# Attention products of a linear-attention and MLP layer: pairs of token tiles in six PSUM banks

## The chip, the core and the metric

The kernel runs on one core of one Trainium2 chip. The metric is device time in microseconds (us). A core has five engines, each with a queue of its own that it works off in order: TensorE (PE in the profile) multiplies matrices into PSUM, ScalarE (ACT) and VectorE (DVE) do elementwise work and are the ones that read PSUM here, GpSimd (POOL) does elementwise work in SBUF, and SyncE (SP) issues the DMAs. PSUM is used as eight banks of 512 fp32 values per partition. The TensorE clock that the profile shows as granted is 1.000 of full speed over the span.

## What is computed

For a sequence of 2048 tokens of 640 features in bf16 the layer adds three things: the input, a linear attention with 32 heads of 20 features, and a gated MLP with 1536 hidden features. Both branches work on the normalized input.

```python
xn = layernorm(x)
q, k, v = heads(xn @ wqkv)                      # 32 heads of 20
phi(u) = [softmax(u @ w_phi), softmax(-u @ w_phi)]   # 40 features per head
kv  = sum over s of phi(k)[s] x v[s]            # 40 x 20 per head
z   = sum over s of phi(k)[s]
o   = (phi(q) @ kv) / (phi(q) . z + 1e-6)
out = x + o @ wo + (silu(xn @ w1) * (xn @ w3)) @ w2
```

## The kernel before

The tokens lie in 16 tiles of 128 (`T`) and four batches of 512 (`NB`). The work on TensorE is cut into units. A unit is a group of matmuls that fills one, two or four neighbouring PSUM banks, followed by the ACT and DVE operations that empty them:

- `v_tile` and `k_tile` (two banks each) make v and exp(plus and minus k) of a token tile, `k_norm` divides the latter by their sums on DVE and POOL, and `kv_sum` and `kv_back` make the matrix of all heads, `KVc`. `KVc` holds 22 columns per head for each sign (`sg`): 20 for the numerator and two for the denominator.
- `q_proj` (one bank, five 512-wide matmuls) makes `EqT`, exp(plus and minus q) of 128 features of a batch, transposed, with two ACT operations.
- `q_tok(t)`, the attention product of token tile t, fills four banks. It runs on half of the array's rows at a time: 20 matmuls of 64 rows and 88 columns. Two with different row halves (`r`) go side by side into different banks. The loops run over sign, over five chunks `c` of the features, and over `r`; bank number 2 x sg + r. ACT then copies the two denominator columns of each head to `e_s` in two operations. DVE makes the products of the parts (`pr_s`), their sum (`den_s`), its reciprocal and the factors `g_s`; one multiply of 1280 elements weights all four banks into `prod`, and that is the last reader of the banks. A further sum gives `o_tok`, which a DMA transposes into `oT` (`turn`). Buffers `e_s`, `pr_s`, `den_s`, `g_s` and `prod` are there twice, by t % 2. A unit may not start before the last multiply of the one before (`u.behind`).
- `mlp(b, fc)` (two banks, 20 matmuls 512 wide) makes 128 hidden features of a batch: ACT makes tanh (`th`), and DVE makes `t1` and `hT` with one operation each.
- `out_tile(t)` (two banks) sums 12 chunks of `hT` by w2 and five of `oT` by wo into the two halves of an output row, 34 matmuls 320 wide. One DVE operation over both banks adds them to `xres`, which holds x, and a DMA stores it. The last tile is cut into 384 and 256 columns instead.

The order of the work is not written out by hand. `schedule` plans it before the program is built: it keeps a clock for each engine, gives every operation a duration (`w_act`, `w_tt` and the like), and takes next the unit or operation that can start earliest. Within a slack the higher level wins; `when(us)` turns a wished time into a level. A unit whose array form differs from that of the one before (`mode`: full rows, rows in halves, columns in halves) is charged `MODE`, 0.085 us. With a seed, and up to 175 us of the plan, the slack is drawn at random, so another seed gives another order. `bank_time` and `group_time` say when banks have been emptied, and `fit` chooses between free ones. A unit of four banks that could start soon keeps others from taking its banks (`blocked`). `emit` then turns the planned order into one list per engine, with waits on semaphores.

Two parts of one unit can be planned apart: `v_split` opens a second unit whose `anchor` is the first one, so that it goes on in the same banks. `emit` numbers the semaphores and lets an output store wait for the fourth store before it.

In the run before, the products of all 16 tiles lie between 117.9 and 202 us of the span. Up to about 165 us `mlp` and `q_proj` units lie between them, from there on one output unit after each product. The last batch's `mlp` units fill 225 to 251 us, and four output units end the span. The load of w2 is issued at 107 us, after the last reader of the memory it takes, and that of wo at 57 us.

Memory that the change touches: `e_s` lies in `RV` behind `oT`, `prod` and `o_tok` in `RW` behind `KVc`.

Of the kernel before, what the change touches and what calls it, by code (L numbers as in the profile page):

```python
# [10 lines left out]
D = 640  # L11
H = 32
# [8 lines left out]

ENGINES = ("PE", "ACT", "DVE", "POOL", "SP")
SEM = {"PE": 0.06, "ACT": 0.04, "DVE": 0.04, "POOL": 0.08, "SP": 0.05}
MODE = 0.085
GRAN = 8
BACKLOG = 5.0

# [28 lines left out]
class _Unit:  # L56


    def __init__(self, banks, level, mode):
        self.banks, self.level, self.mode, self.k = banks, level, mode, None  # L60
        self.mms = []
        self.first = {}
        self.readers = [[] for _ in range(banks)]
        self.behind = []
        self.anchor = None
        self.name = ""


class _Program:
# [100 lines left out]


    def schedule(self, start, filler=None, filler_until=0.0, seed=None, shaken=0.0):
        rng = random.Random(seed)

        for n, o in enumerate(self.all):
            o.idx = n
# [32 lines left out]
        bus = 0.0  # L209
        issue = {"ACT": start["ACT"]}  # L210
        queues = {"SP": [], "ACT": []}
        mode = "full"
        owner = [None] * 8
        ready = {e: [] for e in ENGINES}
        ready_u = [u for u in self.units if not u.missing]
# [113 lines left out]
        def group_time(u, k, guess=False):  # L329
            return max(bank_time(k + j, u.first[j].off if j in u.first else 0.0, guess) for j in range(u.banks))  # L330

        def fit(k, n, t):

            if n == 4:
                return 0
            size = 2 * n
            base = k // size * size
            return sum(1 for i in range(base, base + size) if not k <= i < k + n and bank_time(i, 0.0, True) <= t)
# [3 lines left out]
        while left:  # L342
            best = None
            pick = None
            if ready_u:
                t0 = free["PE"]
                slack = 0.12 if seed is None or t0 > shaken else rng.choice((0.03, 0.12, 0.12, 0.3, 0.6))
                blocked = set()
                cands = []
                for u in ready_u:  # L350
                    extra = MODE if u.mode != mode else 0.0
                    u.at = max(unit_time(u), t0 + extra)
                for u in sorted(ready_u, key=lambda u: (-u.level, u.mms[0].idx)):
                    opts = [(u.at, 0, u.anchor.k)] if u.anchor is not None else []
                    for k in range(0, 8, u.banks) if u.anchor is None else ():
                        if blocked & set(range(k, k + u.banks)):
                            continue
                        g = group_time(u, k)
                        if g < 1e8:
                            opts.append((max(g, u.at), fit(k, u.banks, u.at), k))  # L360
                    if opts:
                        x = min(opts)
                        if pick is None or x[0] < pick[0] - slack:
                            pick = (x[0], u, x[2])
                    if u.banks == 4 and u.at <= t0 + 1.0 and not blocked and (not opts or x[0] > u.at + 0.03):
                        k = min((group_time(u, k, True), k) for k in (0, 4))[1]
                        blocked |= set(range(k, k + 4))
                if pick is not None:
                    best = (pick[0], "PE", pick[1], pick[2])
            moved = False  # L370
            for e in ("ACT", "DVE", "POOL", "SP"):
# [1 line left out]
                    continue  # L373
                ts = [(max(issue[e] if o.nbytes and e == "ACT" else free[e], op_time(o, e)), o) for o in ready[e]]
                t = min(x[0] for x in ts)
                w = 0.09 if seed is None or t > shaken else rng.choice((0.03, 0.09, 0.09, 0.2, 0.4))
                t, o = min((x for x in ts if x[0] <= t + w), key=lambda x: (-x[1].level, x[1].idx))
                if len(o.ways) > 1 and o.level > 1.5e6:
                    other = min(max(free[f], op_time(o, f)) + o.ways[f][2] for f in o.ways if f != e)
# [11 lines left out]
            if e == "PE":  # L391
# [22 lines left out]
                if t > t0 + 0.03 + (MODE if x.mode != mode else 0.0):  # L414
                    self.gaps.append((t0, t - t0, x.name))
                x.k = k
                mode = x.mode
                ready_u.remove(x)
                for j in range(x.banks):
                    p = owner[k + j]  # L420
# [73 lines left out]
CENTRED = {0: "ACT", 1: "ACT", 2: "DVE"}  # L494
POOLED = ()
TURNED = ()
SEED = 1138
TRIPLES = ((0, 3, 0, 60), (3, 3, 60, 60), (6, 3, 120, 60), (9, 3, 180, 60), (12, 3, 240, 60), (13, 3, 300, 20))


def bass_parallel_sum__linear_kernel_hedgehog__glu_gated_swiglu__prompt_kernel(
# [26 lines left out]
    def new(name, shape, dtype, offset=None):  # L528
        size = mybir.dt.size(dtype)
        for n in shape[1:]:  # L530
            size *= n
        return P.sbuf(name, shape, dtype, region(size) if offset is None else offset)
# [9 lines left out]
    mv = new("mv", [128, T, 8], f32)  # L542
    mhalf = new("mhalf", [128, 4], f32)
    warm = new("warm", [128, 8], f32)
    pr_s = new("pr_s", [128, 2, 2, H], f32)
    den_s = new("den_s", [128, 2, H], f32)
    g_s = new("g_s", [128, 2, 2, H], f32)
    S64 = new("S64", [128, 3, 64], f32)
    rS64 = new("rS64", [128, 3, 64], f32)
    xnT = new("xnT", [128, DC, S], bf)  # L550
# [31 lines left out]
    RV = region(21568)  # L582
    v2 = new("v2", [128, T, H * 21 + 2], bf, RV)
    oT = new("oT", [128, DC, S], bf, RV)
    e_s = new("e_s", [128, 2, 4, H], f32, RV + 20480)

    RW = region(12800)
    wqkT = new("wqkT", [128, 2 * DC, D], bf, RW)
    KVc = new("KVc", [128, 2, DC, 4 * 22], bf, RW)
    prod = new("prod", [128, 2, 2, D], bf, RW + 1760)  # L590
    o_tok = new("o_tok", [128, 4, D], bf, RW + 6880)
    kvT = new("kvT", [128, 2, 320], bf, RW + 6880 + 3840)
    EqT = [EqT0, EqT1]
# [4 lines left out]
    def bank(k, cols=512, off=0, p0=0, p1=128):  # L598
        return PS[p0:p1, k * 512 + off:k * 512 + off + cols]
# [62 lines left out]
    def w_op(eng, name, args, busy, lat, **kw):  # L662
        return way(eng, name, args, kw, busy, lat)
# [336 lines left out]
    turned = []  # L1000

    def q_tok(t, level):
        b, jj = divmod(t, 4)
        u = P.begin(4, level, "row", "qt")
        u.name = f"qt{t}"
        u.behind.extend(turned[-1:])
        for sg in range(2):
            for c in range(DC):
                for r in range(2):
                    j = 2 * sg + r  # L1010
                    mm(j, lambda k, j=j, c=c: bank(k + j, 88, 66 * c),
                       EqT[b % 2][64 * r:64 * r + 64, sg, c, 128 * jj:128 * jj + 128],
                       KVc[64 * r:64 * r + 64, sg, c, :], c == 0, c == DC - 1, True,
                       0.003 if r == 0 else 0.045)

        def ps(k):
            a = PS[:, k * 512:(k + 4) * 512].rearrange("p (n c) -> p n c", c=512)[:, :, 0:352]
            return a.rearrange("p n (h c) -> p n h c", c=22)
        e = e_s[:, t % 2, :, :]
        up = 2e6  # L1020
        for sg in range(2):
            o = e[:, sg:4 - sg:3 - 2 * sg, :]
            add([w_act(o.rearrange("p c (q h) -> p q h c", h=16),
                       lambda k, sg=sg: ps(k)[:, 2 * sg:2 * sg + 2, :, 20:22], ACT.Copy, 64)],
                [e], [], [2 * sg, 2 * sg + 1], up)
        pr, den, g = pr_s[:, t % 2, :, :], den_s[:, t % 2, :], g_s[:, t % 2, :, :]
        add([w_tt("DVE", pr, e[:, 0:2, :], e[:, 2:4, :], ALU.mult, 64)], [pr], [e], None, up)
        add([w_tt("DVE", den, pr[:, 0, :], pr[:, 1, :], ALU.add, 32)], [den], [pr], None, up)
        add([w_op("DVE", "reciprocal", (den, den), 0.27, 0.36)], [den], [den], None, up)
        add([w_tt("DVE", g, e[:, 2:4, :], den.unsqueeze(1).to_broadcast([128, 2, 32]), ALU.mult, 64)],  # L1030
            [g], [e, den], None, up)
        gq = g.rearrange("p s (q h) -> p (s q) h", h=16)
        p2 = prod[:, t % 2, :, :]
        add([w_tt("DVE", p2.rearrange("p s (q h c) -> p (s q) h c", q=2, c=DH), lambda k: ps(k)[:, :, :, 0:DH],
                  gq.unsqueeze(3).to_broadcast([128, 4, 16, DH]), ALU.mult, 1280)],
            [p2], [g], [0, 1, 2, 3], up)
        turned.append(P.all[-1])
        o = o_tok[:, t % 4, :]
        add([w_tt("DVE", o, p2[:, 0, :], p2[:, 1, :], ALU.add, D, 2)], [o], [p2], None, 5e5)
        turn(oT[:, :, t * 128:(t + 1) * 128], o, 1e5 - t)  # L1040

    nmlp = [0]

# [18 lines left out]
    def out_tile(t, level):  # L1062
        b, ti = divmod(t, 4)
        u = P.begin(2, level, stream="O")
        u.name = f"O{t}"
        chunks = [(hT[b][:, i, ti * 128:(ti + 1) * 128], w2_s, i) for i in range(FC)]
        chunks += [(oT[:, i, t * 128:(t + 1) * 128], wo_s, i) for i in range(DC)]
        r = xres[:, t % 4, :].rearrange("p (b c) -> p b c", c=320)
# [2 lines left out]
            P.all[-1].early = 60.0  # L1071
        if t < T - 1:
            for n, (l, w, i) in enumerate(chunks):
                for q in range(2):
                    mm(q, lambda k, q=q: bank(k + q, 320), l, w[:, i, 320 * q:320 * q + 320], n == 0,
                       n == len(chunks) - 1)
            add([w_tt("DVE", r, lambda k: bank2(k, 320), r, ALU.add, D)], [xres[:, t % 4, :]],
                [xres[:, t % 4, :]], [0, 1], 1e6)
            finish.append(load(out_t[:, t, :], xres[:, t % 4, :], 3e5 - 2 * t))
            return  # L1080
        for q, c0, c1 in ((0, 0, 384), (1, 384, D)):
# [92 lines left out]
    def when(us):  # L1174
        return 1000.0 - us
# [30 lines left out]
    for b in range(NB):  # L1206
        for j in range(4):
            t = 4 * b + j
            q_tok(t, when(110 + t))
            if b + 1 < NB:  # L1210
                for fc in range((5 * j + 3) // 4, (5 * j + 8) // 4):
                    q_proj(b + 1, fc, when(110 + t + 0.1 * fc))
    for t in range(T):
        out_tile(t, when(200 + 5 * t))

# [62 lines left out]
```

The softmax here doesn't subtract the row's maximum and nothing guards it: scores larger than these inputs give would overflow.

## Time and profile before

| | us |
|---|---|
| median of five runs | 273.76 (273.36 to 273.97) |
| the profiled execution | 273.76 |
| its span, first to last instruction | 272.0 |
| DVE busy, 117 to 128 us | 9.30 of 11 |
| DVE busy, 152 to 164 us | 10.92 of 12 |
| ACT busy, 117 to 128 us | 7.17 of 11 |
| DVE `prod`, 1280 elements, x16 | 1.491 each |
| DVE sum of an output tile, 640 elements, x15 | 0.825 each |
| DVE reciprocal of 64 elements (`rS`), of 32 (`den_s`) | 0.535, 0.353 |
| ACT `e_s`, 64 elements, x32 | 0.283 each |
| transpose of one `o_tok`, from issue to landing | 2.6 |

A profile row for a matmul shows its whole passage through the array, and neighbours overlap: a 512-wide matmul lasts 379 ns, while the next starts 215 to 216 ns after it. What a stretch of matmuls costs is therefore read from the starts. `PEld` rows are the weight loads that run beside them. In a row of the timeline, several instructions of a kind are merged: its first column is the first start, its second the time from there to the last end. An engine's idle time before a row and what ended it stand in brackets.

### The profile page before, as it was taken

To read this page: it belongs to the slowest core of one execution; us is meant where nothing else is said; L and a number is where in the kernel's file an instruction comes from. 1 tells how busy PE (TensorE), PEld (TensorE's weight loads), DVE (VectorE), ACT (ScalarE), POOL (GpSimd) and SP (SyncE) were. 2 spreads that over 40 slices of the span, in tenths; PEclk is the share of its full clock that TensorE was granted. 3 is DMA by queue.
4 is the path that set the end of the run, shared out by engine and by line. 5 is a ranking of instruction groups with operands and counts; after the bars stand their busy time and mean duration, and the time that the engine had idled before them with its cause. 6 is when DMAs were issued, how large, how long until landed. Compare 5 with 4: busy or idle time off the path is not lost.

```text
span 272.0 us, 5056 instructions
## 1 busy us (share of the span) xinstructions
PE 267.4 (98%) x2080; PEld 159.8 (59%) x2098; DVE 182.6 (67%) x325; ACT 101.8 (37%) x190; POOL 60.9 (22%) x101
## 2 busy tenths in 40 slices
PE   8999999999999999999999999999999999999996
PEld 5746546777754448444444446777677774444774
DVE  4848989999998453688869994777673215666112
ACT  5535826777754541355583354100110002222000
POOL 4320642789999900000000000000000000000000
PEclk9999999999999999999999999999999999999999
DMA  7668996863000000804031111333353122000001
GB/s 222 216 98 281 355 164 122 101 164 126 0 0 2 0 0 10 285 0 50 1 51 24 24 27 29 95 99 98 95 100 86 62 77 70 0 0 0 27 24 48
DMA packets 39975, 21.98 MB, mean 81 GB/s; under 512 B 27024, under 2 KB 39952, under 8 KB 39952
## 3 DMA queue, kind: packets, MB, share of 16 engines
q1 hardware_dynamic: 39376, 21.01, 32.4%
q10 hardware_dynamic: 576, 0.66, 0.7%
q8 instruction: 16, 0.26, 0.4%
q14 instruction: 7, 0.06, 0.1%
HBM read 12.81 MB, written 2.62 MB: 57 GB/s over the span
## 4 chain that ended last, share of the span: by engine, by line
PE 94%; DVE 2%; ACT 2%; issue 1%
PE PS L619 92%; PE PS L1098 2%; ACT EqT L627 2%; DVE t L627 1%; PE PS L814 0%; DVE hT L627 0%; PE PS L867 0%; DVE den_s L627 0%; DVE prod L627 0%; ACT e_s L627 0%; DVE g_s L627 0%; DVE xres L627 0%; DVE o_tok L627 0%; DVE pr_s L627 0%
## 5 line engine op out<-in xcount | busy, mean ns | idle before, releaser
L619 PE MATMUL PS<-xnT,w_s 128*128 128x512 bf16 x465 | 104.6, 379 | 1.0 <-issue 0.3
L619 PEld LDWEIGHTS PS<-xnT,w_s 128*128 128x128 bf16 x480 | 46.5, 98 | 54.7
L627 ACT ACTIVATE th<-PS 128x512 f32<-128x512 f32 x48 | 28.7, 597 | 72.0 <-PE PS L619 71.9
L619 PE MATMUL PS<-w_s,hT 128*128 128x320 bf16 (+2 forms) x384 | 55.0, 299 | 0.0
L627 DVE SCALAR_TENSOR_TENSOR t<-th,PS 128x512 bf16<-128x512 f32 x48 | 32.7, 683 | 27.5 <-ACT th L627 27.5
L619 PEld LDWEIGHTS PS<-w_s,hT 128*128 128x128 bf16 x384 | 37.0, 98 | 14.9
L627 POOL TENSOR_TENSOR ekt<-ekt,rS 128x640 bf16<-128x640 bf16 x32 | 39.4, 1264 | 1.1 <-DVE rS L627 1.1
L627 DVE TENSOR_TENSOR xres<-PS,xres 128x640 bf16<-128x640 f32 (+2 forms) x17 | 13.3, 785 | 37.8 <-PE PS L619 37.8
L627 DVE SCALAR_TENSOR_TENSOR hT<-t,PS 128x512 bf16<-128x512 bf16 x48 | 32.7, 684 | 1.3
L627 ACT ACTIVATE EqT<-PS 128x512 bf16<-128x512 f32 x40 | 21.9, 594 | 11.8 <-PE PS L619 11.7
L619 PE MATMUL PS<-wo_s,oT 128*128 128x320 bf16 (+2 forms) x160 | 24.5, 299 | 0.0
L627 DVE TENSOR_TENSOR prod<-PS,g_s 128x1280 bf16<-128x1280 f32 x16 | 23.9, 1491 | 0.6
L627 ACT ACTIVATE ekt<-PS 128x640 bf16<-128x640 f32 x32 | 20.8, 701 | 9.0 <-PE PS L619 8.8
L619 PE MATMUL PS<-Wkp,xnT 128*128 128x320 bf16 x160 | 23.9, 299 | 0.0
L627 ACT ACTIVATE e_s<-PS 128x64 f32<-128x64 f32 x32 | 9.1, 283 | 38.2 <-PE PS L619 37.7
L619 PE MATMUL PS<-xnT,Wqp 128*128 128x512 bf16 x97 | 22.9, 379 | 0.3 <-ACT EqT L627 0.2
L627 DVE TENSOR_REDUCE S<-ekt 128x64 f32<-128x1280 bf16 x16 | 22.9, 1447 | 0.0
L619 PE MATMUL PS<-wv,xnT 128*128 128x320 bf16 x130 | 19.8, 299 | 0.0
L619 PEld LDWEIGHTS PS<-wo_s,oT 128*128 128x128 bf16 x160 | 15.7, 98 | 6.1
L619 PEld LDWEIGHTS PS<-Wkp,xnT 128*128 128x128 bf16 x160 | 15.5, 98 | 5.9
L619 PEld LDWEIGHTS PS<-xnT,Wqp 128*128 128x128 bf16 x100 | 9.4, 98 | 11.0
L627 DVE BATCH_NORM_STATS2 bst<-x_tok 128x6 f32<-128x320 bf16 x32 | 14.1, 469 | 2.6 <-DMA x_tok<-in_A_x_dram 2.6
(66 smaller groups left out, 164.4 us busy)
## 6 DMA issues: line engine op xcount, KB each, us to landing
w_s<-in_B_w_dram SPq DMA_DIRECT2D x6, 640.0 KB, 6.8
xres<-in_A_x_dram SPq DMA_DIRECT2D x16, 160.0 KB, 2.3
out_dram<-xres SPq DMA_DIRECT2D x15, 160.0 KB, 1.8
x_tok<-in_A_x_dram SPq DMA_DIRECT2D x3, 640.0 KB, 8.2
w_s<-in_B_w_dram SPq DMA_DIRECT2D x1, 1920.0 KB, 9.0
wo_s<-in_A_wo_dram SPq DMA_DIRECT2D x1, 800.0 KB, 5.2
x_tok<-in_A_x_dram SPq DMA_DIRECT2D x2, 160.0 KB, 3.6
x_tok<-in_A_x_dram ACTq DMA_DIRECT2D x2, 160.0 KB, 4.0
```

The costliest lines, as they stand in the source:

```text
L619: return nc.tensor.matmul(o(u.k), l, r, start=start, stop=stop, skip_group_check=shared)
L627: return getattr(e, name)(*[at(a, u) for a in args], **{k: at(v, u) for k, v in kw.items()})
L1098: return nc.tensor.matmul(bank(u.k, n), ones[:, 0:128], ones[:, 0:n], start=True, stop=True)
```

## The change

The change has five parts.

1. `q_tok` handles two neighbouring token tiles and is called for every second one. It fills six banks: for tile m of the pair, the bank 2 x r + m holds 23 heads of row half r (16 of one sign and 7 of the other), and the remaining 9 heads of both tiles lie in bank 4 + r. So a chunk of features in which the heads change banks is cut into 22 and 66 columns, and a pair of tiles takes 44 matmuls instead of 40. ACT copies the denominator columns in three operations (128, 56 and 72 elements), DVE makes each small step once for both tiles (`g_s` in two), and three multiplies of 920, 920 and 720 elements each empty two banks. The buffers for these steps are there once. The sums and the transposes stay one per tile.
2. The planner places six banks at 0 to 5 or 2 to 7. Right after a unit of six banks (`wide`) it prefers units that are marked `long`, which are the output units.
3. The output unit of tile 0 (`PARTED`) is planned in two parts: 24 matmuls by w2, and then, in the same banks, ten by wo.
4. The sum of an output tile is two DVE operations of 320 elements, one for each bank, instead of one of 640.
5. `MODE` is 0.096. The levels of `q_tok`, and of the `q_proj` units that are planned with it, go from `when(110 + t)` to `when(118 + 2.5 * t)`. The random draws follow seed 1138 up to 45 us, as before, and seed 597 from there.

```diff
-MODE = 0.085
+MODE = 0.096
...
+        def places(n):
+            return range(0, 9 - n, n if n < 4 else 8 - n)
+
         def fit(k, n, t):
 
-            if n == 4:
+            if n >= 4:
                 return 0
...
-                for u in sorted(ready_u, key=lambda u: (-u.level, u.mms[0].idx)):
+                for u in sorted(ready_u, key=lambda u: (-u.level - (1e7 if wide and u.long else 0), u.mms[0].idx)):
...
-                mode = x.mode
+                mode, wide = x.mode, x.banks == 6
...
-SEED = 1138
+SEED = ((0.0, 1138), (45.0, 597))
+PARTED = (0,)
...
     def q_tok(t, level):
+
         b, jj = divmod(t, 4)
-        u = P.begin(4, level, "row", "qt")
+        u = P.begin(6, level, "row", "qt")
         u.name = f"qt{t}"
         u.behind.extend(turned[-1:])
+        seen = set()
         for sg in range(2):
-            for c in range(DC):
-                for r in range(2):
-                    j = 2 * sg + r
-                    mm(j, lambda k, j=j, c=c: bank(k + j, 88, 66 * c),
-                       EqT[b % 2][64 * r:64 * r + 64, sg, c, 128 * jj:128 * jj + 128],
-                       KVc[64 * r:64 * r + 64, sg, c, :], c == 0, c == DC - 1, True,
-                       0.003 if r == 0 else 0.045)
...
+            for m in range(2):
+                for c in range(DC):
+                    parts = ((0, 4),) if not sg or c != 2 else ((0, 1), (1, 4))
+                    for lo, hi in parts:
+                        for r in range(2):
+                            h = 3 * c + lo
+                            j, off = (4 + r, 256 * m + 22 * (h - 7)) if sg and h >= 7 else (2 * r + m, 22 * (16 * sg + h))
+                            first = j not in seen
+                            seen.add(j)
+                            n = 22 * (hi - lo)
+                            mm(j, lambda k, j=j, n=n, off=off: bank(k + j, n, off),
+                               EqT[b % 2][64 * r:64 * r + 64, sg, c, 128 * (jj + m):128 * (jj + m) + 128],
+                               KVc[64 * r:64 * r + 64, sg, c, 22 * lo:22 * hi], first,
+                               sg == 1 and (c == 2 and hi == 1 if j < 4 else m == 1 and c == DC - 1), True,
+                               0.003 if r == 0 else max(0.024, n / 2400))
...
+        for r in range(2):
+            o, i = prod[:, 2 * r:2 * r + 2, 0:23, :], g_s[:, 2 * r:2 * r + 2, 0:23]
+            add([w_tt("DVE", o, lambda k, r=r: big(k)[:, 2 * r:2 * r + 2, :, 0:DH],
+                      i.unsqueeze(3).to_broadcast([128, 2, 23, DH]), ALU.mult, 920)], [o], [i], [2 * r, 2 * r + 1], up)
+        o, i = prod[:, :, 23:32, :], g_s[:, :, 23:32]
+        add([w_tt("DVE", o, lambda k: rest(k)[:, :, :, 0:DH], i.unsqueeze(3).to_broadcast([128, 4, 9, DH]), ALU.mult,
+                  720)], [o], [i], [4, 5], up)
         turned.append(P.all[-1])
...
+        u.long = True
...
+                if n == FC and t in PARTED:
+                    P.begin(0, u.level).name = f"O{t}b"
+                    P.unit.anchor = u
...
-            add([w_tt("DVE", r, lambda k: bank2(k, 320), r, ALU.add, D)], [xres[:, t % 4, :]],
-                [xres[:, t % 4, :]], [0, 1], 1e6)
+            if P.unit is not u:
+                P.unit.mms[0].war.add(u.mms[-1])
+            last, P.unit = P.unit.mms[-1], u
+            for q in range(2):
+                o = r[:, q, :]
+                add([w_tt("DVE", o, lambda k, q=q: bank(k + q, 320), o, ALU.add, 320)], [o], [o], [q], 1e6, [last])
...
-            q_tok(t, when(110 + t))
+            if j % 2 == 0:
+                q_tok(t, when(118 + 2.5 * t))
             if b + 1 < NB:
                 for fc in range((5 * j + 3) // 4, (5 * j + 8) // 4):
-                    q_proj(b + 1, fc, when(110 + t + 0.1 * fc))
+                    q_proj(b + 1, fc, when(118 + 2.5 * t + 0.1 * fc))
```

## The prediction

> **What bounds the kernel now.** I read the busy shares first, then the chain that ended last, then the start times of matmuls around one attention product, then its chain on ACT and DVE.
>
> ```profile
> PE 267.4 (98%) x2080; PEld 159.8 (59%) x2098; DVE 182.6 (67%) x325; ACT 101.8 (37%) x190; POOL 60.9 (22%) x101
> ...
> PE 94%; DVE 2%; ACT 2%; issue 1%
> ```
>
> TensorE is busy for 98% of the span and carries 94% of the final chain. A busy share does not exclude lost time inside pipelined matmuls, so I compared start times. From 14 us to the end, a 512-wide matmul follows the one before it after 215.5 ns and a 320-wide one after 136 ns, almost without exception. Where twice that appears, a weight load without its matmul shows a record missing, not an idle array. What is left is the change into and out of the 64-row products. The timeline of 170 to 176 us shows one (a row's second column is from its first start to its last end):
>
> ```profile
> 169.82 0.30 PE L619 MATMUL PS<-wo_s,oT 128*128 128x320 bf16 x1
> ...
> 170.05 0.57 PE L619 MATMUL PS<-KVc,EqT 64*128 64x88 bf16 x20
> ...
> 170.55 3.43 PE L619 MATMUL PS<-w_s,hT 128*128 128x320 bf16 x24
> 170.66 0.60 ACT L627 ACTIVATE e_s<-PS 128x64 f32<-128x64 f32 x2 [4.04 <-PE PS L619]
> ...
> 171.29 0.23 DVE L627 TENSOR_TENSOR pr_s<-e_s 128x64 f32<-128x64 f32 x1 [0.31 <-ACT e_s L627]
> 171.55 0.19 DVE L627 TENSOR_TENSOR den_s<-pr_s 128x32 f32<-128x32 f32 x1
> 171.78 0.35 DVE L627 RECIPROCAL den_s<-den_s 128x32 f32<-128x32 f32 x1
> 172.16 0.23 DVE L627 TENSOR_TENSOR g_s<-e_s,den_s 128x64 f32<-128x64 f32 x1
> 172.42 1.49 DVE L627 TENSOR_TENSOR prod<-PS,g_s 128x1280 bf16<-128x1280 f32 x1
> ```
>
> The last wo matmul starts at 169.82 and would be followed after 0.136; the product starts at 170.05, or 0.096 late by the unrounded records. One row matmul takes 202 ns, so the twenty starts lie in 0.57 - 0.20 = 0.36 us: ten pairs, 39.4 ns apart. The last starts at 170.41 and the next full-array matmul 0.134 later, so 0.095 is lost again. All 16 products show both losses, within a nanosecond or two: 16 x 0.191 = 3.06 us.
>
> **Fewer changes of array form: a gain of 1.53 us.** One product for two tiles halves the visits: 8 x 0.191 = 1.53 us. They all lie on TensorE, which waits for nothing else here, so nothing becomes late next.
>
> **More row matmuls: a loss of 0.23 us, at most 0.63.** A pair of tiles had 40 row matmuls, 20 concurrent pairs. It will have 44: per tile, the chunk that crosses the banks' border (sg 1, c 2) is split into 22 and 66 columns. The trace has no 22-wide one. By 66 / 2400 + 0.0025 the wide part takes 30 ns. For the narrow part the nearest rows are the 40-wide pairs of the key-value sum, 24 to 25 ns apart, and from above the 88-wide pairs, 39.4. The Trainium skill, "TensorEngine Tiling (Array Packing)", section Instruction Overhead, speaks against such splitting: each matmul has some 60 cycles of overhead, and a free size of 1 costs as much as 60. Sixty columns are 25 ns at the 0.42 ns of the 512-wide row. Read per instruction, a product would take 44 x 25 = 1.10 us instead of the 0.79 of two now, an added 8 x 0.31 = 2.5 us that would eat the gain. The row denies it for concurrent tiles: twenty matmuls start in 0.36 us, 20 ns each, under that floor. So I count the floor once for a concurrent pair: 2 x (24 + 30 - 39.4) = 29 ns, x 8 = 0.23 us. With every pair at 39.4 the two added ones cost 79 ns a product, x 8 = 0.63 us.
>
> **Six banks instead of four: a loss of 0.5 us, between 0 and several.** Here the change can lose. Before, the product left four banks to others; now it leaves two until its first multiply ends. I build the release from the rows above, counted from the start of the last row matmul. ACT begins 0.25 later (170.66 against 170.41). Two e_s copies of 64 elements take 0.60; the three new ones have 128, 56 and 72. The ACT rows of 512 and 64 elements, 597 and 283 ns, give 0.7 ns an element, so I estimate 0.33 + 0.28 + 0.29 and small gaps, 0.95. The small steps follow: pr at 128 elements 0.29 (0.225 plus 64 / 960), den 0.22, the 64-wide reciprocal 0.535 (the rS row), two multiplies for g 0.37, with gaps 1.5. The first of three multiplies, 920 instead of 1280 wide, takes 1.49 - 0.375 = 1.12. With 0.06 for the semaphore, its two banks come free at about 3.9 us, the next two 1.0 and the last two 0.8 later.
>
> TensorE is covered for 0.134 plus one unit in the other two banks. The new rule in the planner prefers an output unit after a wide product. A whole one is 34 x 0.136 = 4.62 us, so it covers until 4.76: 0.85 to spare. An MLP unit is 20 x 0.2155 = 4.31, until 4.45: 0.5 to spare. But the first wide product has no finished attention tile behind it, so the unit after it is the split one, cut before wo: 24 x 0.136 = 3.27 us, until 3.40. Its two banks stay taken until the transposed output has landed, so nothing can start before 3.9: **a hole of 0.5 us, once**. The planner may not see it: it gives an e_s copy 0.113 us of ACT time where the trace shows 0.30, so three copies come about 0.45 us later than it plans. With four spare banks that error cost nothing. I take 0.5, from the sum; the other ends are 0 (another unit was left free) and the starvation below.
>
> In front of a wide product six banks must be free. Two units earlier is over 4 us ago, and DVE and ACT drain a unit within about 1.4, so I count nothing.
>
> **Output sums by bank: nothing.** 15 sums of 640 (0.825 each, 12.4 us in all) become two of 320, about 0.48 each, starting 0.40 apart by the element rate. The unit after a wide product reuses the banks of the output unit before it. The sum starts 0.11 after the product's first matmul (170.16 against 170.05), so the banks free at 0.65 and 1.05; a wide product occupies TensorE for 20 x 0.0394 + 0.03 + 0.095 = 0.91, and the second bank's first matmul comes 0.136 later, at 1.05. One sum of 640 would free both at 0.99, 0.08 late, for some seven products: without this part 0.5 us would be lost. With it the fit is tight, plus or minus 0.1 each at most.
>
> **DVE, ACT, SyncE: nothing by themselves.** Two tiles cost DVE 2 x (0.23 + 0.19 + 0.35 + 0.23 + 1.49 + 0.49) = 5.96; now about 5.6. ACT has three e_s copies for four. DVE is 9.3 of 11 us busy from 117 to 128 and 10.9 of 12 from 152 to 164, so it isn't idle, but the saving only eases it. The transposes stay 16, now issued in twos, each 1.21 us of SyncE and 2.6 to landing; the x loads and stores queued behind a second one come 1.2 us later. The output unit of tile k stands about k wide products after that of tile 0, while its oT is made after product k / 2, so that cover is several units long.
>
> **Levels and seed: nothing, or a loss.** Products get later levels, and from 45 us the planner draws other numbers. An order without holes can't be improved by another order, only spoiled. The opening and the last unit keep their work. The switch cost in the planner, 0.085, becomes 0.096, what the trace shows, which only makes the plan truer.
>
> **Sum**, against the profiled execution: span 272.0, 1.76 around it, 273.76, the same as the median. -1.53 + 0.23 + 0.5 = -0.8: **272.96 us**.
>
> **Rivals.**
> 1. No hole at all: -1.53 + 0.23 = -1.3, **272.46**. For it: not one hole shows after 14 us now. Against: the split unit is shorter than the release.
> 2. Bank starvation, the slower side. The chain of a wide product meets one EqT on ACT (594 ns, as at 128.93, where the copies waited for it) and one t or hT on DVE (0.69): release at 5.2 instead of 3.9, past even a whole output unit by 0.45. In every second product that costs 4 x 0.45 = 1.8 beside the first hole: 273.76 - 0.8 + 1.8 = **274.8**; in every one, with 1.3 more in the first, 277.4. It decides from a mean of 1.3 / 8 = 0.16 us a product. For it: DVE near 90% busy in this stage, and the plan's too short copies. The skill warns likewise (same page, PSUM Bottleneck: draining PSUM can become the bound once tiles speed up TensorE). Against: products before followed such collisions without a hole, though with more banks.
> 3. It cancels: a few holes of 0.1 to 0.3 at tight places, or the narrow matmuls at their upper price with one hole and 0.4 elsewhere: -1.53 + 0.63 + 0.5 + 0.4 = 0.0, **273.76**.
>
> **Chances.** What a measurement can tell from no change is 0.2%, 0.55 us. The forecast (one hole) has 0.38, rival 1 0.20, rival 3 0.20, rival 2 0.22. Faster by more than that: the forecast less 0.02 that falls into the band, and rival 1, 0.36 + 0.20 = 0.56; within: 0.20 + 0.02 = 0.22; slower: 0.22. The range runs from 272.3 (rival 1 and a little) to 274.9, to take in the milder starvation; the likeliest case alone is 272.6 to 273.3.
>
> **What would show it.** Eight groups of 44 row matmuls with 0.095 on each side; 54 ns, not 79, for each split chunk; the wait of TensorE for the first prod after the first wide product, about 0.5 us, with e_s taking some 0.95; elsewhere 512- and 320-wide starts at 215 and 136 ns. Waits of TensorE for prod after most products would make the prediction wrong, and so would a hole in front of a wide product, while other banks drain.

## The result and the profile after

| | before | after |
|---|---|---|
| median, us | 273.62 (48 runs, 272.97 to 274.18) | 273.03 (27 runs, 272.43 to 274.88) |
| profiled execution, us | 273.76 | 272.86 |
| its span, us | 272.0 | 271.0 |
| start of the key-value sum on TensorE, us | 103.71 | 103.42 |
| from there to the start of the last matmul, us | 165.54 | 164.77 |

The ratio of the times is 0.9982 with a 95% interval of 0.9976 to 0.9989: 0.5 us faster, between 0.3 and 0.66. That is just inside the 0.2% that was called no change ahead of the runs, and the interval reaches beyond it. Two more sets of runs of the same kernel, below, gave 0.9987 (0.9979 to 0.9995) and 0.9992 (0.9977 to 1.0006).

The last row of the table is the measure that the experiments rest on. All work ahead of the key-value sum is as before, but it waits for the first DMAs, so the sum's start moves by some tenths from one execution to the next. Behind it the same kernel repeats within 0.16 us, and there the change is worth 0.77 us. All of the 0.16 lies within the sum itself, in one trace (e8): counted from the sum's last matmul, the three traces of the changed kernel have 160.06 or 160.07 us and the kernel before 160.83.

The page of the changed kernel, busy shares and the chain that ended last:

```profile
PE 266.2 (98%) x2114; PEld 159.8 (59%) x2130; DVE 179.4 (66%) x322; ACT 102.1 (38%) x184; POOL 60.8 (22%) x101
...
PE 97%; ACT 1%; issue 1%; DVE 0%
```

There are 34 matmul records more (32 more are issued; the other two are records missing before), and yet 1.2 us less of busy TensorE. TensorE still sets the end; the DVE work that shared the chain before is gone from it, and one per cent of ACT is left. The chain in order of time, between 125 and 175 us, shows where it comes from (start, duration, what):

```profile
128.48 1.04 PE PS L627 x4
129.52 0.02 issue
129.54 1.09 ACT EqT L635 x2
130.63 0.05 issue
130.68 14.52 PE PS L627 x118
...
152.74 1.09 ACT EqT L635 x2
```

At two places the chain leaves TensorE for two EqT operations: TensorE waited for a bank that they drained. The timeline around the first and the second six-bank product:

```profile
127.33 0.99 PE L627 MATMUL PS<-KVc,EqT 64*128 64x88 bf16 x44
127.43 1.08 ACT L635 ACTIVATE EqT<-PS 128x512 bf16<-128x512 f32 x2 [1.56 <-PE PS L627]
128.40 1.03 ACT L635 ACTIVATE e_s<-PS 128x128 f32<-128x128 f32 x3
128.48 4.54 PE L627 MATMUL PS<-xnT,Wqp 128*128 128x512 bf16 x19 [0.16 <-issue]
...
129.54 2.16 ACT L635 ACTIVATE EqT<-PS 128x512 bf16<-128x512 f32 x4
...
131.15 2.95 DVE L635 TENSOR_TENSOR prod<-PS,g_s 128x920 bf16<-128x920 f32 x3
131.97 2.16 ACT L635 ACTIVATE EqT<-PS 128x512 bf16<-128x512 f32 x4 [0.27 <-PE PS L627]
...
139.42 0.99 PE L627 MATMUL PS<-KVc,EqT 64*128 64x88 bf16 x44
139.80 0.69 DVE L635 SCALAR_TENSOR_TENSOR hT<-t,PS 128x512 bf16<-128x512 bf16 x1
140.34 3.50 PE L627 MATMUL PS<-w_s,hT 128*128 128x320 bf16 x24
...
143.68 1.52 PE L627 MATMUL PS<-wo_s,oT 128*128 128x320 bf16 x10
```

The 44 row matmuls last 0.99 from the first start to the last end; the next unit starts 0.92 after, at 140.34, behind the second one. (Behind the first one a record is missing.) Behind the first product stand q units, and not, as predicted, the first output unit. That one follows the second product, and its two parts run one behind the other: 24 matmuls by w2 from 140.34, ten by wo from 143.68.

The account goes by the starts of all matmuls from the key-value sum on. A visit is the change to the row form and back with the row matmuls between, and a hole is the time by which a matmul starts later than the 0.216 us (512 columns) or 0.136 us (320) after the one before it. Two visits took 1.188 us of TensorE before, and the one for a pair takes 1.018 now: eight times 0.170 is 1.36 us saved. Behind every visit, before and after, the second full-array matmul starts another 0.010 late; half the visits save eight of these, 0.08. Against that stand four holes, 0.65 us. Two of 0.262 lie between q units (at 130.4 and 153.6), two of 0.065 after the first matmul of an output unit (140.4 and 163.6). Before, there was none. The sum is -1.36 - 0.08 + 0.65 = -0.79, beside the table's -0.77. None of the four waits for `prod`: the first two end when EqT has emptied a bank, the others when hT has (139.80 + 0.69 = 140.49, and the matmul starts at 140.54).

### The profile page after: what moved, and what is told of

It reads as the page before. It is cut to its first block, busy times and chain, and to the rows that moved or that the text cites. A ratio compares the mean times of both kernels' runs of the same rounds, so it can differ in the third digit from the quotient of the medians.

```text
span 271.0 us, 5106 instructions
## 1 busy us (share of the span) xinstructions
PE 266.2 (98%) x2114; PEld 159.8 (59%) x2130; DVE 179.4 (66%) x322; ACT 102.1 (38%) x184; POOL 60.8 (22%) x101
## 4 chain that ended last, share of the span: by engine, by line
PE 97%; ACT 1%; issue 1%; DVE 0%
PE PS L627 95%; PE PS L1134 2%; ACT EqT L635 1%; PE PS L875 0%; PE PS L822 0%; DVE xres L635 0%
## 5 line engine op out<-in xcount | busy, mean ns | idle before, releaser
L635 DVE TENSOR_TENSOR xres<-PS,xres 128x320 bf16<-128x320 f32 (+2 forms) x32 | 14.3, 484 | 35.4 <-PE PS L627 35.4
L635 ACT ACTIVATE e_s<-PS 128x128 f32<-128x128 f32 (+2 forms) x24 | 7.7, 319 | 44.8 <-PE PS L627 44.2
L635 DVE TENSOR_TENSOR prod<-PS,g_s 128x920 bf16<-128x920 f32 (+1 forms) x24 | 23.6, 1040 | 0.3
```

Source lines behind the costliest of these rows:

```text
L635: return getattr(e, name)(*[at(a, u) for a in args], **{k: at(v, u) for k, v in kw.items()})
```

## The experiments

The theory: the gain is the saved visits alone, less the dearer product, and the loss is that six banks are taken at once. Its rivals were that sums, order or the cut unit bring the gain or the loss, and that late `e_s` copies make the holes. All times below are device times, with the ratio to the kernel before on the same chip. "Stretch" is the time from the start of the key-value sum to that of the last matmul. The medians of e6, e7, e9 and the repeats differ by no more than their noise, so what these runs say rests on the starts in their traces, one for each run.

| kernel | median, us | ratio to before (95%) | stretch, us |
|---|---|---|---|
| e1, before with sums by bank | 273.58 | 0.9993 (0.9985 to 1.0001) | - |
| e2, each product in two visits | 274.79 | 1.0034 (1.0024 to 1.0044) | 166.52 |
| e3, no preference for output units | 275.27 | 1.0054 (1.0041 to 1.0066) | 166.73 |
| e4, output units half by half | 272.91 | 0.9968 (0.9958 to 0.9978) | 164.37 |
| e5, all but the pairs | 273.91 | 1.0003 (0.9994 to 1.0013) | 165.61 |
| e6, one sum of 640, same order | 273.71 | 0.9998 (0.9988 to 1.0007) | 165.03 |
| e7, no cut unit | 273.63 | 0.9994 (0.9983 to 1.0005) | 165.14 |
| e8, changed again | 273.53 | 0.9987 (0.9979 to 0.9995) | 164.92 |
| e9, two copies on DVE | 273.13 | 0.9987 (0.9974 to 1.0001) | 164.77 |
| e10, half by half again | 272.47 | 0.9961 (0.9947 to 0.9975) | 164.37 |
| e11, changed, third time | 273.26 | 0.9992 (0.9977 to 1.0006) | 164.76 |

### What brings the gain: e1, e5 and e2

e1 puts one part of the change into the kernel before:

```diff
-            add([w_tt("DVE", r, lambda k: bank2(k, 320), r, ALU.add, D)], [xres[:, t % 4, :]],
-                [xres[:, t % 4, :]], [0, 1], 1e6)
+            last = P.unit.mms[-1]
+            for q in range(2):
+                o = r[:, q, :]
+                add([w_tt("DVE", o, lambda k, q=q: bank(k + q, 320), o, ALU.add, 320)], [o], [o], [q], 1e6, [last])
```

> The kernel before with one part of the change alone: output sums in two operations of 320, one per bank; TensorE's order stays. Theory (the gain is the eight saved visits to the 64-row form, and the sums only fit the six-bank product): no change, 273.6, within 0.15, and sums of 0.48 each, 0.40 apart. Rival (part of the gain comes from the sums): 0.3 us or more faster.

Measured: 273.58 beside 273.80, 0.9993, with 1 inside the interval. The rival's 0.3 us (0.9989) lies inside the interval too, so this run alone does not shut it out. Its trace can't decide: the profiled execution took 1594.93 us, with 1.70 us for a 512-wide matmul instead of 0.379, for a reason that isn't known.

e5 is the other way round: the changed kernel with the whole product function of before and its buffers. Three of its lines:

```diff
-        u = P.begin(6, level, "row", "qt")
+        u = P.begin(4, level, "row", "qt")
...
-            if j % 2 == 0:
-                q_tok(t, when(118 + 2.5 * t))
+            q_tok(t, when(118 + 2.5 * t))
```

> The changed kernel with the attention product of before: one token tile in four banks, 16 visits, with its own buffers; the sums by bank, the split unit, the new levels, seed and planned switch cost stay. Theory (the pairs alone carry gain and loss): no holes and 16 visits, so the time of the kernel before, within 0.15 us. Rival (order, levels or sums bring part of the gain): 0.3 us or more faster than before.

Measured: 1.0003, and a stretch of 165.61 beside 165.54 (0.08 is one product that starts late, behind the `prod` of the one before). Sums, cut, levels, seed and the planner's switch cost together bring nothing. The gain is the pairs'.

e2 doubles the visits of the changed kernel and leaves the rest in its order:

```diff
             for m in range(2):
+                if sg and m:
+                    mm(4, lambda k: bank(k + 4, 48, 460), ident[:], ident[:, 0:48], False, False, True, 0.0)
                 for c in range(DC):
```

> The changed kernel with each product cut in two visits: one full-array matmul of 48 columns into unused columns of the product's fifth bank stands in the middle of the 44 row matmuls; order and output stay. Theory (a visit costs what the starts show, 0.096 in and 0.091 out): 8 x (0.096 + 0.091 + 0.025) = 1.7 us slower than the changed kernel, 1.6 if the small holes swallow some, so about 274.6, 1.0 above the kernel before. Rival (the visit's cost is mostly overlapped, and the gain is from elsewhere): at most 0.3 slower than the changed kernel.

Measured: a stretch of 166.52, 1.75 more than the changed kernel's 164.77; the median is 1.0 us above the kernel before, as expected. The timeline of e2 shows one of the eight cuts:

```profile
183.74 0.78 PE L627 MATMUL PS<-KVc,EqT 64*128 64x88 bf16 x32
184.45 0.20 PE L627 MATMUL PS<-ident 128*128 128x48 bf16 x1
184.58 0.38 PE L627 MATMUL PS<-KVc,EqT 64*128 64x88 bf16 x12
184.90 1.80 PE L627 MATMUL PS<-w_s,hT 128*128 128x320 bf16 x12
```

The 48-column matmul starts 0.130 after the row matmul before it, and the row matmuls go on 0.129 after its start. Of these 0.26 us, 0.04 and 0.02 are the two matmuls' own, so the two changes of form cost 0.20. By all starts, a cut product takes 1.253 us instead of 1.018: these 0.20, the 0.02 of the added matmul and 0.015 in the starts behind it. Eight times 0.235 is 1.88; the two holes of 0.065 vanish, which leaves the measured 1.75. The price of a visit is real time of TensorE, and the rival falls.

### What makes the holes: e3, e9 and e6

e3 takes the preference for output units away:

```diff
-        u.long = True
+        u.long = False
```

> The changed kernel without the preference for output units after a six-bank product; the order is planned anew. Theory (six banks starve TensorE unless a unit of 3.9 us or more covers the product's chain): after products that are followed by an MLP unit (ten matmuls, 2.16 us) holes of up to 1.4 us appear, some 2 us more of holes in all, so about 274.8, slower than the kernel before. Rival (the banks don't matter, any unit covers): within 0.3 of the changed kernel's 273.0.

Measured: 275.27, and a stretch of 166.73, 1.96 us above the changed kernel. Its holes sum to 2.60 us instead of 0.65, which is the difference. The largest, in its timeline:

```profile
151.22 0.99 PE L627 MATMUL PS<-KVc,EqT 64*128 64x88 bf16 x44
...
152.36 2.11 PE L627 MATMUL PS<-xnT,Wqp 128*128 128x512 bf16 x9 [0.16 <-issue]
...
153.43 2.17 ACT L635 ACTIVATE EqT<-PS 128x512 bf16<-128x512 f32 x4
...
155.04 2.14 DVE L635 TENSOR_TENSOR prod<-PS,g_s 128x920 bf16<-128x920 f32 x2
155.65 1.69 PE L627 MATMUL PS<-xnT,w_s 128*128 128x512 bf16 x7 [1.18 <-ACT EqT L635]
```

Two q units take the two free banks. The next unit, an MLP one, needs both, and the second is drained only when the fourth EqT ends at 155.60. The product's own first banks would be free only later, since its first multiply starts at 155.04. Another hole, 0.73 us up to 143.56, lies behind a product with an MLP unit behind it: a q unit waits until that unit's `t` has emptied its first bank. So the holes of 0.7 to 1.4 came, but the largest in another way than expected: it takes two q units and a unit of two banks. TensorE starves, and the change becomes a loss, as in the prediction's slower rival; but no hole waits for `prod`, as that rival had it. What keeps the starvation off is the order.

e9 moves two of the three copies to DVE. The plan, and so TensorE's order, keeps the old durations:

```diff
-            add([w_act(o, src, ACT.Copy, free(o))], [e_s[:]], [], js, up)
+            y = w_act(o, src, ACT.Copy, free(o))
+            if free(o) < 128:
+                y = way("DVE", "tensor_copy", (o, src), {}, *w_copy(o, src, free(o))[1][1:])
+            add([y], [e_s[:]], [], js, up)
```

> The changed kernel with the e_s copies of 56 and 72 elements on DVE instead of ACT; the order of TensorE stays. Theory (the holes of 0.26 us are a bank's turn: 0.2 from a q unit's last matmul to its first EqT, 1.08 for two EqT, 0.06 back, against the 1.08 of the one other q unit that can run): both holes stay at 0.26, and so does the time of the changed kernel within 0.15. Rival (ACT is late because three copies take 1.03 us instead of the planned 0.50, as the prediction feared): ACT is freed 0.6 earlier, and the holes shrink below 0.1, 0.3 to 0.5 us faster.

Measured: the stretch stays at 164.77 and both holes at 0.262. Its timeline:

```profile
128.34 0.40 ACT L635 ACTIVATE e_s<-PS 128x128 f32<-128x128 f32 x1
...
128.77 0.57 DVE L635 COPY e_s<-PS 128x56 f32<-128x56 f32 x2 [1.52 <-ACT e_s L635]
...
129.47 2.16 ACT L635 ACTIVATE EqT<-PS 128x512 bf16<-128x512 f32 x4 [0.73 <-PE PS L627]
...
131.90 1.08 ACT L635 ACTIVATE EqT<-PS 128x512 bf16<-128x512 f32 x2 [0.27 <-PE PS L627]
```

ACT now sits idle for 0.73 us ahead of the EqT operations, and they start no earlier: it is the q unit's last matmul that lets them start. So late copies are not the cause. The hole is a bank's turn. In the changed kernel the last matmul of the first q unit behind the product starts at 129.12 (the record of its first one is missing), EqT starts 0.42 later (129.54), two of them take 1.09, and TensorE goes on at 130.68, 1.56 after that matmul. The matmul itself takes 0.216 of this, and in between there is only one other q unit, five matmuls in 1.08. That leaves 0.26. The 0.2 in the expectation is counted from the end of the 0.216, and comes to the same.

e6 takes back the sums by bank, with everything else in place:

```diff
             for q in range(2):
                 o = r[:, q, :]
-                add([w_tt("DVE", o, lambda k, q=q: bank(k + q, 320), o, ALU.add, 320)], [o], [o], [q], 1e6, [last])
+                if q == 0:
+                    y = w_tt("DVE", o, lambda k, q=q: bank(k + q, 320), o, ALU.add, 320)
+                    z = way("DVE", "tensor_tensor", (r, lambda k: bank2(k, 320), r, ALU.add), {}, y[1][1], y[1][2])
+                else:
+                    y = w_tt("DVE", o, lambda k, q=q: bank(k + q, 320), o, ALU.add, 320)
+                    z = way("DVE", "memset", (S64[:, 0, t:t + 1], 0.0), {}, y[1][1], y[1][2])
+                add([z], [o], [o], [q], 1e6, [last])
```

> The changed kernel with the sum of an output tile done by one operation of 640 over both banks again; a memset of one unused column stands where the second sum stood, so the order of every engine stays. Theory (a fit to within 0.1 us): four of the eight products stand between two output units; there the next unit's first bank comes free at 0.99 us after the product's start instead of 0.65, while TensorE is done after 0.92, so four holes of about 0.07, 0.3 us in all, 273.3. Rival (the sums have slack): the changed kernel's time, no holes there.

Measured: 165.03, 0.26 us above the changed kernel, by four holes of 0.065: each of the four products between two output units takes 1.083 instead of 1.018. The two timelines at the same product, first the changed kernel:

```profile
182.97 0.99 PE L627 MATMUL PS<-KVc,EqT 64*128 64x88 bf16 x44
183.07 0.89 DVE L635 TENSOR_TENSOR xres<-PS,xres 128x320 bf16<-128x320 f32 x2 [3.73 <-PE PS L627]
183.89 3.43 PE L627 MATMUL PS<-w_s,hT 128*128 128x320 bf16 x24
```

and e6:

```profile
182.79 0.99 PE L627 MATMUL PS<-KVc,EqT 64*128 64x88 bf16 x44
182.90 0.82 DVE L635 TENSOR_TENSOR xres<-PS,xres 128x640 bf16<-128x640 f32 x1 [3.79 <-PE PS L627]
...
183.78 3.43 PE L627 MATMUL PS<-w_s,hT 128*128 128x320 bf16 x24
```

The output unit comes 0.92 after the product's start with two sums and 0.99 with one. In the changed kernel the first sum ends at 183.56, in time for 183.89; the second ends at 183.96, and the matmul into its bank starts at 184.03, with no more than the 0.010 that stands behind every product. The part of the change that looks idle by itself (e1) is worth 0.26 us once the product lies between two output units.

### The order: e7, e8 and e11

e7 has no cut unit (`PARTED = ()`).

> The changed kernel without the cut of the first output unit ahead of wo; the order is planned anew and differs from about 145 us on. In the changed kernel the two parts ran one right behind the other, so on the chip the cut changed no instruction's place by itself. Theory: only the planned order differs, with holes of 0.26 three times and 0.065 to 0.1 twice instead of twice and twice, so 0.2 to 0.3 us slower than the changed kernel. Rival (the cut gives cover that is needed): a hole of 0.5 us or more after the first product with an output unit behind it.

Measured: a stretch of 165.14. Counted from the sum's last matmul that is 160.44, 0.37 above the changed kernel. Its holes are 0.26 twice, 0.25, 0.16, 0.06 and 0.02. The one of 0.16 lies at the start of a six-bank product, where the changed kernel loses nothing:

```profile
152.75 1.67 ACT L635 ACTIVATE EqT<-PS 128x512 bf16<-128x512 f32 x3
...
153.24 1.15 PE L627 MATMUL PS<-KVc,EqT 64*128 64x88 bf16 x44
```

The first row matmul starts at 153.24 and the second, which needs another bank, at 153.40, just after an EqT ends at 153.35; so the product takes 1.15 instead of 0.99. The one of 0.25 stands at 173.2, where an output unit's second matmul waits for the bank of an MLP unit. The product behind which the cut unit stood in the changed kernel has no hole of 0.5 here. In the changed kernel the two parts ran one behind the other anyway. So the cut acts through the plan alone.

> The changed kernel once more, beside the kernel before on the same chip, as a reference for the other three. Theory: 0.5 to 0.7 us faster than before, the same holes of 0.26 and 0.065 us twice each to within 0.02, and a start of the key-value sum that moves by some tenths of a us from execution to execution, as the DMAs of the opening land. Rival (the holes are chance): other holes.

> The changed kernel as the reference for the two others. Theory: 0.4 to 0.7 us faster than before, from the start of the key-value sum to the last matmul 164.8 us, against 165.5 before; what an execution differs by lies ahead of that. Rival: the stretch behind that start itself varies by more than 0.2 us.

Measured: 0.4 and 0.2 us faster than before by the ratios, less than the 0.5 to 0.7 and 0.4 to 0.7 that were expected. The holes are 0.262 twice and 0.061 to 0.065 twice in both, the stretches 164.92 and 164.76 against 164.77. The start of the key-value sum is 104.03 and 104.32 instead of 103.42. DVE's rows in the opening show why, in the first trace of the changed kernel

```profile
6.26 1.43 DVE L635 BATCH_NORM_STATS2 bst<-x_tok 128x6 f32<-128x320 bf16 x3
...
7.84 0.39 DVE L635 TENSOR_SCALAR xc<-x_tok,mv 128x640 bf16<-128x640 bf16 x1
```

and in e8:

```profile
6.74 0.89 DVE L635 BATCH_NORM_STATS2 bst<-x_tok 128x6 f32<-128x320 bf16 x2 [0.56 <-DMA x_tok<-in_A_x_dram]
7.99 0.49 DVE L635 BATCH_NORM_STATS2 bst<-x_tok 128x6 f32<-128x320 bf16 x1 [0.37 <-DMA x_tok<-in_A_x_dram]
...
8.63 0.39 DVE L635 TENSOR_SCALAR xc<-x_tok,mv 128x640 bf16<-128x640 bf16 x1
```

The statistics of an early x tile wait 0.9 us for its DMA, and the centred tile comes 0.8 later; TensorE's start of the key-value sum moves by 0.6. The whole times of the three traces, 272.86, 273.46 and 273.85, follow these starts to 0.1 us, so most of the spread of the runs seems to lie there. It also hides part of the gain: 0.77 us in the stretch, and 0.2 to 0.5 in the three ratios. Whether the changed kernel's opening is later on average can't be said, since there is one trace of the kernel before.

### A version that beats both: e4 and e10

Each output unit fills its first bank with 17 matmuls, sums it, and then fills the second. The plan knows the copies' measured durations, no unit is cut, and the seed is another one:

```diff
-SEED = ((0.0, 1138), (45.0, 597))
+SEED = ((0.0, 1138), (45.0, 150))
...
+        for q, c0, c1 in ((0, 0, 320), (1, 320, D)) if t < T - 1 else ((0, 0, 384), (1, 384, D)):
+            for n, (l, w, i) in enumerate(chunks):
+                mm(q, lambda k, q=q, c=c1 - c0: bank(k + q, c), l, w[:, i, c0:c1], n == 0, n == len(chunks) - 1)
+            o = xres[:, t % 4, c0:c1]
+            add([w_tt("DVE", o, lambda k, q=q, c=c1 - c0: bank(k + q, c), o, ALU.add, c1 - c0)], [o], [o], [q], 2e6 if t == T - 1 else 1e6)
...
```

> The changed kernel with output units worked half by half (17 matmuls into the first bank, its sum, then 17 into the second), e_s durations in the plan as measured, no part before wo, seed 150 from 45 us. Theory (0.66 us of holes are left: twice 0.26 where three q units follow each other in the two free banks, twice 0.065 where an output unit's second matmul waits for the bank of an MLP unit): the two of 0.065 vanish, since the second bank is first needed 2.3 us later, and one of about 0.27 is left, so 0.35 to 0.4 us faster than the changed kernel, 272.65. Rival (the holes are set by something else than banks, such as late e_s copies): holes of the same total, 273.0.

> The kernel with output units worked half by half once more, beside the changed kernel on the same chip. Theory: one hole of 0.26 instead of 0.66 us of holes, so 0.35 to 0.4 us faster than the changed kernel and 0.8 to 1.1 faster than the kernel before. Rival (the difference between the two earlier sets of runs was the chip's): no difference from the changed kernel.

Measured: 0.9968 and 0.9961, 0.9 and 1.1 us faster than before; on one chip 272.47 beside the changed kernel's 273.26. The stretch is 164.37 both times, 0.40 below the changed kernel. One hole of 0.262 is left, between q units. In e4's timeline an output unit follows a product that follows an MLP unit:

```profile
136.91 0.99 PE L628 MATMUL PS<-KVc,EqT 64*128 64x88 bf16 x44
137.29 0.69 DVE L636 SCALAR_TENSOR_TENSOR hT<-t,PS 128x512 bf16<-128x512 bf16 x1
137.83 1.80 PE L628 MATMUL PS<-w_s,hT 128*128 128x320 bf16 x12
```

hT ends at 137.98, and the second bank is first asked for 2.3 us behind 137.83. Which of the edits removed the other hole between q units (the seed or the durations) was not separated.

## Why the prediction was right, and where it was not

The predicted time, 272.96, is close to the measured 273.03, and the predicted change in the execution, -0.8, to the -0.77 of the stretch. The gain came as forecast. The loss came near in size, but not by the wait that the prediction described. Point by point:

- **Fewer changes of form, -1.53, and more row matmuls, +0.23.** Right: -1.36 together against -1.30. The way in still costs 0.096, the way out 0.091 where it was 0.095. The prediction left out the 0.010 at the second matmul behind each visit, which brings another 0.08. e2 and e5 show that nothing else brings the gain. The split chunks take 30 and 29 ns instead of the 24 and 30 that were assumed, so the least time counts once for two matmuls side by side, not once for each as the rule of the Trainium skill (TensorEngine Tiling (Array Packing), Instruction Overhead) can be read; the 20 ns a matmul in the trace before had said so. The 2400 columns per us in that sum are the slope between the starts of 512- and 320-wide matmuls (0.216 and 0.136), and the 960 elements per us in others that between DVE rows of 1280 and 640 elements (1.491 and 0.825).
- **Six banks, +0.5 as one hole behind the first product.** The wait was wrong, and that the size is near is luck. The prediction had TensorE wait for the product's own first multiply, behind the split unit. "The unit after it is the split one" failed: behind the first and third product stand q units. And TensorE never waited for `prod`. The two banks that are left came round too slowly: 0.262 twice for a bank that EqT empties, and 0.065 twice, behind the second and fourth product, for the second bank of an MLP unit. Together 0.65.
- **Late copies.** The prediction feared that the plan's short durations would tell. The three copies take 1.03 us against 0.50 planned, and yet in e9, with two of them on DVE, the holes are the same.
- **A wrong size in the prediction and in the description of the kernel:** an MLP unit is ten matmuls, five for each of two weights, 2.16 us and not 4.31. So it does not cover the 4.2 us that the first two banks take to come free (from 128.12, the last row matmul's start, to 131.15 + 1.12, and the semaphore; 3.9 was predicted). This is one reason why the preference for output units matters as much as e3 shows.
- **Starvation, as the slower rival.** Not in the changed kernel, but real in another order: e3, at 275.27, is a little above the 274.8 of that rival. Its path, a release of the product at 5.2 us for which TensorE waits, shows in no trace with six banks; e3's holes wait for EqT and `t`. One product of e3 does give up its first banks only 5.0 us behind its last row matmul (140.52 to 144.40 + 1.11), but TensorE has a unit to work on until then.
- **In front of a product nothing.** Right in the changed kernel: no product starts late. In e7's order one loses 0.16, so a product can have to wait for its banks where units just before it still drain. The second bank of the unit behind it was late by 0.065 where an MLP unit went before, because hT ends 0.15 after that unit's start (140.49 against 140.34).
- **Sums by bank.** Right, with 0.065 instead of 0.08 us, and four places instead of seven.
- **Levels and seed: nothing, or a loss.** Right: e5 gains nothing, and in e7 another order costs 0.37.
- **The chances.** 0.56 was put on more than 0.2% faster. The three ratios lie at 0.08 to 0.18%, so the case that came, by that bound, is "within".

## What to carry to other kernels

Where one engine is busy throughout, count what it pays at changes of form from the starts of its instructions, and expect to get back nearly all of it by fewer visits. A larger visit takes more buffers at once: before making it, compare the time until the first of them comes free with the longest unit that fits into what is left, and with the turn of a single buffer (fill, drain, signal), since where two units fit, a third can still wait for the buffer of the first. When a plan orders the work, judge a change by the trace from the first point that does not depend on the opening's DMAs.

## What was not expected of the hardware

- Two concurrent 64-row matmuls of 22 columns hold TensorE as long as two of 66: 30 and 29 ns, against 38.5 to 39 for 88. From 66 to 22 columns nothing was saved.
- Small ACT copies out of PSUM did not overlap: three of 128, 56 and 72 elements took 0.40, 0.27 and 0.30 us and 1.03 together, with 0.03 between them, and the one of 128 is longer than the 0.33 that the slope between 64 and 512 elements gives. Two DVE sums of 320 in a row started 0.40 to 0.41 apart while each lasted 0.48, so those did.
